# Attention inputs laid out by numpy ahead of a windowed-attention and mixture-of-experts kernel

## The chip, the cores and the metric

The kernel runs on one core of one Trainium2 chip. The metric is the device time of one execution in microseconds. The comparison is with the kernel before the change, of which three timed runs and one profiled execution are at hand. What numpy does to the inputs before the launch and to the output after it is not in the device time.

## The reference

Three layers follow one another. The first is attention with 4 batches, 8 heads, 576 positions and 64 features to a head. Heads 0 to 3 see the last 32 positions, heads 4 to 7 see every fourth of the last 128. The second layer is a mixture of 8 experts that takes 2304 tokens of 512 features, picks two experts for each token by noisy logits and sums their outputs. The third is a dense pair of matrices with a softmax gate and a normalization between them.

```python
scores = scale * np.matmul(q, k.transpose(0, 1, 3, 2))
rel = pos[:, None] - pos[None, :]
mask_plain = (rel >= 0) & (rel < 32)
mask_dil = (rel >= 0) & (rel < 128) & (rel % 4 == 0)
scores = np.where(masks, scores, -1e9)
attn = np.exp(scores - max); attn = attn / (attn.sum + 1e-9)
x = np.matmul(attn, v)                       # (4, 8, 576, 64) -> 2304 tokens x 512

logits = x @ w_gate
noisy = logits + np.log1p(np.exp(x @ w_noise)) * noise
top2 = the two largest of 8
out[t] = sum over top2 of weight * (relu(x[t] @ w1[e]) @ w2[e])

h = out @ w_in
solu = h * softmax(h)
y = layernorm(solu) * g_ln @ w_out
```

The dilated heads read every fourth position. If positions are sorted by their remainder modulo 4 (their class, 144 positions each), the dilated window becomes a plain window of 32 neighbours inside a class. Both kinds of head are then computed by the same code on blocks of 64 queries and 96 keys, with a mask.

## The kernel before

**Attention.** A *pair* j is two heads of one batch; there are 16 of them, four to a batch, in the order of heads given by `HPS`. A pair has three *groups* of three blocks of 64 queries, so there are 48 groups. For group g the kernel runs these steps:
- `scores(g)` on PE: two matmuls add the mask (L191), twelve matmuls multiply queries and keys (L196), into one of two PSUM buffers `s`;
- `soft_a(g)`: DVE takes the maxima (L203), ACT the exponentials with their sums (L207);
- `soft_0(g)` and `soft_b(g)`: DVE adds 1e-9 and takes the reciprocal (L212, L217), POOL multiplies (L219, tile `pn`);
- `ptrans(g)`: PE transposes the probabilities (L226), ACT copies them out of PSUM (L228);
- `pv(g)`: twelve matmuls with the values (L243), and `evac` copies the result into `xt` on DVE (L263), one copy for a plain pair, two for a dilated one.

The loop over g is a software pipeline written out by hand: iteration g issues `scores(g + 2)`, `ptrans(g - 1)` and `pv(g - 2)` on PE in this order, and each engine works through its own instructions in program order.

**Inputs.** q and k come from DRAM as rows of 64 features (`load_qk`, four transfers to a pair, L139, tile `nat`). `trans(j, part)` turns them: four parts to a pair, each of three PE transposes of 96 columns (L167); ACT copies the keys out (L177), DVE the queries with the scale (L179), into `qkt`, which has room for two pairs. For dilated pairs the copy also sorts positions by class. The table `TD` puts two parts each into the second and third iteration of a pair. v comes in rows of 64 features too (`load_v`, L147 for plain heads, L155 for dilated ones, tile `vwt`); a block needs 96 keys, of which 32 are the last ones of the block ahead, and `share_v` copies these on POOL (L160). All these loads are issued on SP's queue.

**Beside the groups.** From g = 15 on, `gate(n)` computes a tile of 128 tokens for the router: six matmuls or more into `ga_a`, two into `ga_b` (L288), and the rows are stored to DRAM (L303). From g = 23 on, the router's DVE work (`front`, `rank`) is spread over the iterations from a list `bg` by a table of costs, and from g = 26 on the first expert's weights are split in two parts by ACT and POOL (L564, L567). 13 of the 18 gates stand inside the loop. After it come the other gates, the second half of the routing, and then the experts (L610), which begin at about 161 us and fill PE from about 180 us to the end.

Of the kernel before, what the change touches and what calls it, by code (L numbers as in the profile page):

```python
# [24 lines left out]
W = 32  # L25
# [8 lines left out]
N1 = 9  # L34
NR = 9
# [7 lines left out]
TD = ((), ((2, 0), (2, 2)), ((2, 1), (2, 3)))  # L43
# [13 lines left out]
XE_ = lambda g: g > 50  # L57
# [3 lines left out]
def const_arrays():  # L61
# [20 lines left out]
    bits = (masks.reshape(128, -1).view(np.uint32) >> 16).astype(np.uint16)  # L82
    return {"masks": bits, "cpack": pk}

# [6 lines left out]
def tile_kernel(ctx, tc, q, k, v, w_gate, w_noise, noise, w1, w2, w_in, w_out, g_ln, masks, cpack, out, stop=None):  # L91
# [33 lines left out]
    qk = big.tile([128, 2, 2 * S + W], F32, name="qkt", tag="ha")  # L125
    QT = [qk[:, i, :S] for i in range(2)]
    KT = [qk[:, i, S:] for i in range(2)]
    NAT = {}
    XT = {}

    def load_qk(j, halves=(slice(0, 6),)):
        b, hp = j // 4, HPS[j % 4]
        if j not in NAT:
            NAT[j] = big.tile([128, 2, 6, 2 * D], F32, name="nat", tag=("x0", "x1h", "x1l")[j % 3])
        o = (b * H + 2 * hp) * S * D
        for g in halves:
            for i, src in enumerate((q, k)):
                for h in range(2):
                    nc.sync.dma_start(NAT[j][:96, i, g, D * h:D * h + D],  # L139
                                      dram_ap(src, o + (h * S + g.start * 96) * D,  # L140
                                              [[D, 96], [96 * D, g.stop - g.start], [1, D]]))

    def load_v(b, d, i0=0, i1=NBLK):
        o = (b * H + 4 * d) * S * D
        if d == 0:
            for h in range(4):
                nc.sync.dma_start(VW[0][W:, i0:i1, h], dram_ap(v, o + (h * S + 64 * i0) * D,  # L147
                                                               [[D, 64], [64 * D, i1 - i0], [1, D]]))
            return
        u = 64 * i0  # L150
        while u < 64 * i1:
            c = u // NCLS
            e = min(64 * (u // 64 + 1), (c + 1) * NCLS)
            p0 = W + u % 64
            nc.sync.dma_start(VW[1][p0:p0 + e - u, u // 64],  # L155
                              dram_ap(v, o + (DIL * (u - c * NCLS) + c) * D, [[DIL * D, e - u], [S * D, 4], [1, D]]))
            u = e

    def share_v(d, i0, i1):
        nc.gpsimd.tensor_copy(VW[d][:W, i0 + 1:i1 + 1], VW[d][64:64 + W, i0:i1])  # L160

    def trans(j, part):
        hp = HPS[j % 4]
        nm, a = part // 2, part % 2
        ps = psum.tile([128, 288], F32, name="tr", tag="t")
        for g in range(3):
            nc.tensor.transpose(ps[:, 96 * g:96 * g + 96], NAT[j][:96, nm, 3 * a + g], idf[:96, :96])  # L167
        if hp < 2:
            src = ps
            place = lambda t: t[:, 288 * a:288 * a + 288]  # L170
        else:
            src = ps.rearrange("p (i c) -> p c i", c=4)
            place = lambda t: t.rearrange("p (c i) -> p c i", c=4)[:, :, 72 * a:72 * a + 72]

        def evac():
            if nm == 1:
                nc.scalar.copy(place(KT[j % 2][:, W:]), src)  # L177
            else:
                nc.vector.tensor_scalar(place(QT[j % 2]), src, scale, None, op0=OP.mult)  # L179

        return evac
# [707 lines left out]
    for p_ in (0, 2):  # L889
        trans(0, p_)()  # L890
# [288 lines left out]
```

## Time and profile before

| what | value |
|---|---|
| median of 3 runs | 861.88 us (861.49 to 861.94) |
| the profiled execution's own time | 860.89 us |
| span of its trace | 859.1 us |
| PE busy | 827.4 us, 96% of the span |
| DVE, ACT, POOL busy | 531.7, 337.6 and 197.1 us |
| TensorE clock granted, mean | 0.985 |

The profiled execution's time is 1.8 us more than the span, and 1.0 us less than the median. Shares of busy time over the whole span say little about the first 150 us, where attention runs and the limits change from stage to stage. The rows that matter are therefore those of stretches of that part. Groups are numbered here from 0, and a group's start is the start of its mask matmuls (L191).

### The profile page before, as it was taken

How to read it: one execution, taken by the hardware profiler on the slowest of the kernel's cores; microseconds unless marked ns; L12 is line 12 of the kernel's file. 1: busy time of each engine (PE TensorE's matmuls, PEld its weight loads, DVE VectorE, ACT ScalarE, POOL GpSimd, SP SyncE). 2: the span in 40 equal slices, each digit the busy share in tenths (PEclk: the TensorE clock that was granted, in tenths of full speed). 3: DMA queues.
4: the chain of work that ended last, by engine and by line, in shares of the span. 5: the costliest groups of instructions: out<-in, count | busy, mean ns of one | idle time of the engine just before them, and what ended most of it. 6: DMA issues, size and time to landing. Idle time of an engine off the chain costs nothing.

```text
span 859.1 us, 14969 instructions
## 1 busy us (share of the span) xinstructions
PE 827.4 (96%) x5588; PEld 722.5 (84%) x5588; DVE 531.7 (62%) x1289; ACT 337.6 (39%) x862; POOL 197.1 (23%) x212
## 2 busy tenths in 40 slices
PE   6999888999999999999999999999999999999997
PEld 4877767889998998988989989889987888888886
DVE  2656688735475564755855755341656878777883
ACT  2767757424332322432323223331534433443332
POOL 3533557351101001011010020011314222212200
PEclk9999969899999999999999999999999999999999
DMA  7668774334445525545455364252522222122101
GB/s 167 127 131 195 181 182 132 112 97 130 133 158 172 184 91 192 167 142 170 149 193 170 101 197 148 67 154 75 160 76 84 74 74 61 56 68 74 39 25 40
DMA packets 113470, 106.23 MB, mean 124 GB/s; under 512 B 65744, under 2 KB 86256, under 8 KB 113392
## 3 DMA queue, kind: packets, MB, share of 16 engines
q1 hardware_dynamic: 107248, 85.25, 34.3%
q0 software_dynamic: 6144, 19.96, 7.9%
q8 instruction: 46, 0.75, 0.4%
q14 instruction: 32, 0.26, 0.1%
HBM read 81.00 MB, written 24.19 MB: 122 GB/s over the span
## 4 chain that ended last, share of the span: by engine, by line
PE 86%; DVE 6%; DMA 3%; SPq 2%; ACT 1%; issue 1%; POOL 0%; POOLq 0%; ACTq 0%; DVEq 0%
PE l L610 51%; PE fh L738 11%; PE fo L610 10%; PE xtp L597 2%; DMA nat<-in_k_dram 2%; PE pv L243 2%; PE s L196 2%; PE fzp L756 2%; PE tr L167 2%; PE pt L226 2%; PE ga_a L288 1%; SPq L139 1%; SPq L147 1%; PE xtp L676 1%; PE s L191 1%
## 5 line engine op out<-in xcount | busy, mean ns | idle before, releaser
L580 POOL DMA_INDIRECT xg<-xs,idx x40 | 46.3, 1158 | 329.7 <-PE xtp L597 323.3
L610 PE MATMUL l<-x,w1h 128*128 128x256 f32 x512 | 95.4, 285 | 0.0
L610 PE MATMUL l<-x1h,w1h 128*128 128x384 f32 x256 | 85.9, 335 | 0.0
L610 PE MATMUL l<-x1l,w1h 128*128 128x384 f32 x256 | 85.8, 335 | 0.0
L610 PE MATMUL l<-x1h,w1l 128*128 128x384 f32 x256 | 85.6, 335 | 0.0
L610 PEld LDWEIGHTS l<-x,w1h 128*128 128x128 f32 x512 | 83.1, 193 | 0.6
L610 PE MATMUL l<-w2h,h1h 128*128 128x512 f32 x192 | 76.8, 400 | 0.0
L610 PE MATMUL l<-w2h,h1l 128*128 128x512 f32 x192 | 75.1, 391 | 0.0
L610 PE MATMUL l<-w2l,h1h 128*128 128x512 f32 x192 | 74.9, 390 | 0.0
L610 PE MATMUL l<-x,w1l 128*128 128x256 f32 x256 | 72.9, 285 | 0.0
L631 DVE SCALAR_TENSOR_TENSOR h1l<-l,h1h 128x384 fp32r<-128x384 f32 x64 | 35.4, 553 | 47.2 <-ACT h1h L630 47.1
L630 ACT ACTIVATE h1h<-l 128x384 fp32r<-128x384 f32 x64 | 31.4, 491 | 83.0 <-PE l L610 83.0
L567 DVE TENSOR_TENSOR w1l<-raw,w1h 128x1024 fp32r<-128x1024 f32 x32 | 38.3, 1230 | 28.1 <-ACT w1h L564 28.1
L650 DVE COPY yo<-l 128x512 f32<-128x512 f32 x22 | 15.2, 692 | 64.6 <-PE l L610 64.6
L207 ACT ACTIVATE p<-s,ng 128x96 f32<-128x96 f32 x144 | 47.2, 339 | 14.7 <-DVE r L212 9.0
L610 PE MATMUL fo<-w2x,fz 128*128 128x512 f32 (+1 forms) x228 | 52.8, 379 | 0.0
L610 PE MATMUL l<-w2h,h0h 128*128 128x512 f32 x128 | 50.8, 397 | 0.0
L630 ACT ACTIVATE h0h<-l 128x256 fp32r<-128x256 f32 x58 | 22.3, 384 | 71.3 <-PE l L610 71.0
L738 PE MATMUL fh<-w1h,fx 128*128 128x512 f32 x144 | 49.1, 403 | 1.2 <-ACT fx L682 0.7
L610 PE MATMUL l<-w2h,h0l 128*128 128x512 f32 x128 | 50.1, 391 | 0.0
L670 POOL TENSOR_TENSOR yg<-yg 128x512 f32<-128x512 f32 x18 | 23.2, 1292 | 116.8 <-ACT yg L669 116.8
L610 PE MATMUL l<-w2l,h0h 128*128 128x512 f32 x128 | 50.0, 390 | 0.0
(204 smaller groups left out, 2023.6 us busy)
## 6 DMA issues: line engine op xcount, KB each, us to landing
raw<-in_moe_w_dram SPq DMA_DIRECT2D x64, 512.0 KB, 3.9
ys<-yo SPq DMA_DIRECT2D x40, 256.0 KB, 2.1
out_dram<-yo SPq DMA_DIRECT2D x17, 256.0 KB, 2.0
nat<-in_q_dram SPq DMA_DIRECT2D x30, 144.0 KB, 3.5
nat<-in_k_dram SPq DMA_DIRECT2D x30, 144.0 KB, 3.7
raw<-in_moe_w_in_dram SPq DMA_DIRECT2D x8, 512.0 KB, 4.1
raw<-in_moe_w_out_dram SPq DMA_DIRECT2D x8, 512.0 KB, 3.7
xs<-xo SPq DMA_DIRECT2D x13, 256.0 KB, 3.7
```

Of the source, the lines that this page charges most:

```text
L167: nc.tensor.transpose(ps[:, 96 * g:96 * g + 96], NAT[j][:96, nm, 3 * a + g], idf[:96, :96])
L196: nc.tensor.matmul(ps[h, i], QT[j % 2][h, u:u + 64], KT[j % 2][h, u:u + 96], start=False, stop=i == 2, skip_group_check=True)
L207: nc.scalar.activation(p[:, i], s[:, i], AF.Exp, bias=ng[:, i:i + 1], accum_out=sm[:, i:i + 1])
L226: nc.tensor.transpose(ps[:, i], pn[:, i], idf)
L243: nc.tensor.matmul(ps[64 * h:64 * h + 64, 64 * i:64 * i + 64], vw[:, 3 * t + i, 2 * (hp % 2) + h, :], pt[:, i, 64 * h:64 * h + 64], start= ...
L567: (eng or nc.vector).tensor_sub(l, r, h.bitcast(F32))
L580: nc.gpsimd.indirect_dma_start(out=t, out_offset=None, in_=xs[:128 * N1] if h == 0 else xs, in_offset=bass.IndirectOffsetOnAxis(ap=idx[:, ...
L610: nc.tensor.matmul(ps, A[x], Bm[y], start=first and i == 0, stop=last and i == 2)
L630: nc.scalar.activation(hh[:, ft], ps, AF.Relu)
L631: nc.vector.scalar_tensor_tensor(hl[:, ft], ps, 0.0, hh[:, ft].bitcast(F32), op0=OP.max, op1=OP.subtract)
L670: nc.gpsimd.tensor_tensor(a, a, b, op=OP.add)
L738: nc.tensor.matmul(ps, FX[n][x][:, kk], W1[y][:, 2 * c:2 * c + 2, kk], start=kk == 0 and i == 0, stop=kk == 3 and i == 2)
```

## The change

Numpy now lays out the inputs before the launch, in `lay_out`:
- q and k are given as one array `kq`: for each pair, 128 rows (two heads of 64 features), each with 576 key positions and then 576 query positions. Dilated heads have their positions sorted by class. `load_kq` brings a pair with one transfer, two pieces of 2304 bytes to a row, into one of four buffers `kq` (before: rows of 256 bytes, transposed on PE).
- v is given as blocks of 96 keys, with the 32 shared keys written out twice. `load_v` brings all nine blocks of four heads with one transfer; `share_v` is gone.
- The order of tokens in the rest of the kernel is by class for all heads. Plain pairs are written to `xt` with a permutation in the `evac` copy, dilated ones with one plain copy. The noise is permuted in the same way, and the output is put back by numpy.
- The identity for the mask matmul is part of the `masks` array, and the gate weights come as one array.

On chip, `trans` and its copies on ACT and DVE are gone. `scale_q` multiplies a pair's queries by the scale in place on DVE, once to a pair, in the iteration of a pair's first group, one pair ahead. A new function `heat` runs matmuls of a tile of ones: 34 ahead of group 0's scores, and 16 after those of group 1. Nothing reads their result.

```diff
+H0, H1 = 34, 16
-TD = ((), ((2, 0), (2, 2)), ((2, 1), (2, 3)))
...
+    KQ = [big.tile([128, W + 2 * S], F32, name="kq", tag=t) for t in ("x0", "x1h", "x1l", "ha")]
+    KT = [t[:, :W + S] for t in KQ]
+    QT = [t[:, W + S:] for t in KQ]
...
+    def load_kq(j, u0=0, u1=S):
+        o = (j // 4 * 4 + HPS[j % 4]) * 128 * 2 * S
+        dst = KQ[j % 4][:, W:].rearrange("p (a s) -> p a s", a=2)[:, :, u0:u1]
+        nc.sync.dma_start(dst, dram_ap(kq, o + u0, [[2 * S, 128], [S, 2], [1, u1 - u0]]))
+
+    def scale_q(j, eng, u0=0, u1=S):
+        eng.tensor_scalar(QT[j % 4][:, u0:u1], QT[j % 4][:, u0:u1], scale, None, op0=OP.mult)
...
+        o = (2 * b + d) * 96 * NBLK * 4 * D
+        nc.sync.dma_start(VW[d][:, i0:i1].rearrange("p i h d -> p (i h d)"),
+                          dram_ap(vw, o + i0 * 4 * D, [[NBLK * 4 * D, 96], [1, (i1 - i0) * 4 * D]]))
...
         if hp < 2:
-            evs = [(x[:, hp, 192 * t:192 * t + 192], ps)]
+            dst = x[:, hp].rearrange("p (c i) -> p c i", c=DIL)[:, :, 48 * t:48 * t + 48]
+            src = ps.rearrange("p (i c) -> p c i", c=DIL)
         else:
...
+            dst, src = x[:, hp, 192 * t:192 * t + 192], ps
...
+    def heat(n):
+        ps = psum.tile([128, 128], F32, name="heat", tag="t")
+        for _ in range(n):
+            nc.tensor.matmul(ps, one, one, start=True, stop=True, skip_group_check=True)
+
+    heat(H0)
+    scale_q(0, nc.vector, 0, 192)
     scores(0)
-    for p_ in (1, 3):
-        trans(0, p_)()
+    soft_a(0)
+    scale_q(0, nc.vector, 192, S)
     scores(1)
-    soft_a(0)
+    heat(H1)
...
-        if t == 0:
+        if t == 0 and j + 1 < 16:
+            scale_q(j + 1, nc.vector)
             if j + 3 < 16:
-                load_qk(j + 3)
-        for dj, p_ in TD[t]:
-            if 2 <= j + dj < 16 and j + dj > 1:
-                ev.append(trans(j + dj, p_))
...
-        if g and vb < 4:
-            if m < 3:
-                load_v(vb, d, 3 * m, 3 * m + 3)
-            else:
-                share_v(d, max(3 * m - 10, 0), 3 * m - 7)
+        if g >= 8 and g % 6 == 2 and g < 45:
+            load_v((g - 8) // 12 + 1, (g - 8) // 6 % 2) if g < 42 else None
```

**PE, one iteration in the middle of a pair.** Before, between a group's scores (`s`) and the transposes of the probabilities (`pt`) stand six transposes of inputs (`tr`):

```order
L191 LDWEIGHTS idb
L191 MATMUL s<-mk,idb 64x288
L191 LDWEIGHTS idb
L191 MATMUL s<-mk,idb 64x288
L196 MATMUL s<-qkt 64x96 x6
L167 MATMUL tr<-cp,nat 128x96 x6
L226 MATMUL pt<-cp,pn 96x128 x3
L243 MATMUL pv<-ptS,vwt 64x64 x6
```

The same iteration of the changed kernel:

```order
L171 LDWEIGHTS mk
L171 MATMUL s<-mk 64x288
L171 LDWEIGHTS mk
L171 MATMUL s<-mk 64x288
L176 MATMUL s<-kq 64x96 x6
L206 MATMUL pt<-cp,pn 96x128 x3
L223 MATMUL pv<-ptS,vwt 64x64 x6
```

The six transposes are gone and the rest stands in the same order (the program lists two matmuls of the two heads as one row).

**DVE, two iterations early in the loop.** Before, each copy of queries out of PSUM (`qkt<-tr`) stands between the copy of a result and the next maxima:

```order
L263 COPY xt<-pv 128x192
L179 TENSOR_SCALAR qkt<-tr 128x4x72
L203 TENSOR_REDUCE ng<-s 128x3
L212 TENSOR_SCALAR r<-sm 128x3
L217 RECIPROCAL r<-r 128x3
L263 COPY xt<-pv 128x192
L179 TENSOR_SCALAR qkt<-tr 128x4x72
L203 TENSOR_REDUCE ng<-s 128x3
```

The changed kernel at the first group of a pair and the one after it:

```order
L232 COPY xt<-pv 128x4x48
L156 TENSOR_SCALAR kq<-kq 128x576
L183 TENSOR_REDUCE ng<-s 128x3
L192 TENSOR_SCALAR r<-sm 128x3
L197 RECIPROCAL r<-r 128x3
L232 COPY xt<-pv 128x4x48
L183 TENSOR_REDUCE ng<-s 128x3
```

Two operations that read PSUM have become one that reads and writes SBUF (`kq<-kq`), and it waits for the transfer of the next pair.

**SP, the loads of the first iterations.** Before:

```order
L147 DMA vwt<-in_v_dram 64x3x64 x4
L139 DMA nat<-in_q_dram 96x6x64 x2
L139 DMA nat<-in_k_dram 96x6x64 x2
L147 DMA vwt<-in_v_dram 64x6x64 x4
L139 DMA nat<-in_q_dram 96x6x64 x2
L139 DMA nat<-in_k_dram 96x6x64 x2
```

In the changed kernel the same part of the queue, from the first blocks of v to the third pair, with the rest of the constants (`cp`) in it:

```order
L160 DMA vwt<-in_vw_dram 96x768
L153 DMA kq<-in_kq_dram 128x1152
L160 DMA vwt<-in_vw_dram 96x1536
L759 DMA cp<-in_cpack_dram 128x316
L153 DMA kq<-in_kq_dram 128x1152
```

Sixteen transfers have become four, and over the whole of attention 160 transfers of q, k and v have become 26.

## Rows read from the trace of the kernel before

**Rows 1.** The page: its first line.

```profile
span 859.1 us, 14969 instructions
```

**Rows 2.** Windows by stage: window, length, busy time of each engine, clock, DMA share, GB/s.

```profile
0.00:24.55 24.55, 16.19 (x126) 12.60 (x126) 6.30 (x22) 8.12 (x33) 7.97 (x20) 1.00 0.78 160
24.55:51.43 26.88, 24.79 (x400) 20.14 (x397) 16.63 (x61) 19.32 (x93) 12.35 (x18) 0.99 0.59 119
51.43:98.36 46.93, 43.61 (x590) 35.80 (x589) 28.81 (x116) 33.24 (x147) 20.25 (x28) 0.97 0.75 170
98.36:145.96 47.60, 41.74 (x541) 34.08 (x541) 39.39 (x153) 30.00 (x126) 30.67 (x33) 0.86 0.66 165
145.96:180.00 34.04, 29.55 (x287) 26.31 (x287) 25.53 (x110) 15.94 (x47) 14.54 (x18) 0.90 0.31 99
```

**Rows 3.** Timeline of PE: start, length, instructions; mask matmuls of groups, two score rows.

```profile
21.35 1.17 PE L196 MATMUL s<-qkt 64*64 64x96 f32 x12
...
24.55 0.31 PE L191 MATMUL s<-mk,idb 64*64 64x288 bf16 x2
...
24.69 0.66 PE L196 MATMUL s<-qkt 64*64 64x96 f32 x12
...
26.24 0.31 PE L191 MATMUL s<-mk,idb 64*64 64x288 bf16 x2
...
28.45 0.31 PE L191 MATMUL s<-mk,idb 64*64 64x288 bf16 x2
...
51.43 0.45 PE L191 MATMUL s<-mk,idb 64*64 64x288 bf16 x2
...
95.48 0.31 PE L191 MATMUL s<-mk,idb 64*64 64x288 bf16 x2
...
98.36 0.31 PE L191 MATMUL s<-mk,idb 64*64 64x288 bf16 x2
...
145.96 0.31 PE L191 MATMUL s<-mk,idb 64*64 64x288 bf16 x2
```

**Rows 4.** The chain that ended last, in order of time: start, length, what.

```profile
15.58 4.10 DMA nat<-in_k_dram
...
44.80 3.77 DMA vwt<-in_v_dram
...
74.28 5.72 DMA nat<-in_k_dram
...
83.08 6.57 DMA nat<-in_k_dram
```

**Rows 5.** Groups by line and form, 0 to 180 us: busy, mean ns, idle before, releasers.

```profile
L167 PE MATMUL tr<-cp,nat 96*128 96x96 f32 x192 | 27.9, 286 | 11.9 <-DMA nat<-in_q_dram 5.5 <-DMA nat<-in_k_dram 5.5 <-DVE qkt L179 0.6
...
L179 DVE TENSOR_SCALAR qkt<-tr 128x288 f32<-128x288 f32 x32 | 14.6, 457 | 30.3 <-PE tr L167 30.1
L160 POOL COPY vwt<-vwt 32x768 f32<-32x768 f32 x16 | 13.0, 813 | 15.8 <-DMA vwt<-in_v_dram 15.2
L177 ACT COPY qkt<-tr 128x288 f32<-128x288 f32 x32 | 12.8, 400 | 9.4 <-PE tr L167 9.4
...
L263 DVE COPY xt<-pv 128x192 f32<-128x192 f32 x24 | 8.3, 344 | 3.2 <-PE pv L243 3.1
...
L263 DVE COPY xt<-pv 128x144 f32<-128x144 f32 x16 | 6.5, 408 | 0.0
...
L263 DVE COPY xt<-pv 128x48 f32<-128x48 f32 x16 | 3.9, 241 | 1.3 <-PE pv L243 1.3
```

**Rows 6.** DMA rates in 40 slices: of 10 to 20 us, then of 210 to 220 us.

```profile
GB/s 92 161 193 218 193 257 256 257 247 211 228 195 204 167 162 120 197 193 116 191 122 157 226 210 219 234 182 251 261 281 263 237 193 183 166 224 236 219 195 208
...
GB/s 393 139 25 16 197 246 311 213 33 82 139 16 74 188 344 328 393 434 426 434 254 33 16 33 0 0 0 0 0 115 180 164 328 238 238 360 402 344 344 279
```

**Rows 7.** DVE on SBUF: a group after 180 us; line 212 alone (min/median/max ns).

```profile
L522 DVE TENSOR_SCALAR nt<-nt 128x512 int32<-128x512 int32 x16 | 6.7, 418 | 0.0
...
L212 DVE TENSOR_SCALAR r<-sm x48: 152/160/1212, 11.1 to 150.0; 128x3 f32<-128x3 f32 x48
```

More of the change, by code (lines that the diff above doesn't have):

```diff
@@ L81, in const_arrays, with by_class, lay_out @@
     pk[:, CP_VAL:CP_VAL + 36] = 128 * (np.arange(36)[None, :] // 2) + r[:, None] - TOK0
-    bits = (masks.reshape(128, -1).view(np.uint32) >> 16).astype(np.uint16)
+    masks = np.concatenate([np.eye(128, dtype=np.float32), masks.reshape(128, -1)], 1)
+    bits = (masks.view(np.uint32) >> 16).astype(np.uint16)
     return {"masks": bits, "cpack": pk}
+def by_class(a, axis):
+    s = a.shape
+    a = a.reshape(s[:axis] + (NCLS, DIL) + s[axis + 1:])
+    return np.ascontiguousarray(np.swapaxes(a, axis, axis + 1)).reshape(s)
+def lay_out(given):
+    q, k, v, noise = (given.pop(n) for n in ("q", "k", "v", "moe_noise"))
+    half = lambda a: np.concatenate([a[:, :H // 2], by_class(a[:, H // 2:], 2)], 1)
+    kq = np.stack([half(a).reshape(B, H // 2, 2, S, D).transpose(0, 1, 2, 4, 3) for a in (k, q)], 4)
+    vp = np.pad(half(v), ((0, 0), (0, 0), (W, 0), (0, 0)))
+    rows = 64 * np.arange(NBLK)[None, :] + np.arange(96)[:, None]
+    vw = vp[:, :, rows].reshape(B, 2, 4, 96, NBLK, D).transpose(0, 1, 3, 4, 2, 5)
+    nz = by_class(noise.reshape(B, S, E), 1).reshape(NT, 128, E).transpose(1, 0, 2)
+    wg = np.stack([given.pop(n) for n in ("moe_w_gate", "moe_w_noise")], 1).reshape(4, 128, 16).transpose(1, 0, 2)
+    given.update(kq=kq.reshape(B * H // 2, 128, 2 * S), vw=vw.reshape(B * 2, 96, NBLK * 4 * D),
+                 noise=nz.reshape(128, NT * E), gates=wg.reshape(128, 64))
 def dram_ap(t, offset, dims):
@@ L90, in tile_kernel @@
 @with_exitstack
-def tile_kernel(ctx, tc, q, k, v, w_gate, w_noise, noise, w1, w2, w_in, w_out, g_ln, masks, cpack, out, stop=None):
+def tile_kernel(ctx, tc, kq, vw, gates_w, noise, w1, w2, w_in, w_out, g_ln, masks, cpack, out, stop=None):
     nc = tc.nc
@@ L143, in load_v @@
-    def load_v(b, d, i0=0, i1=NBLK):
[L144 to L157, printed above, removed]
@@ L195, in scores @@
             for h in hd:
-                nc.tensor.matmul(ps[h, i], QT[j % 2][h, u:u + 64], KT[j % 2][h, u:u + 96], start=False,
+                nc.tensor.matmul(ps[h, i], QT[j % 4][h, u:u + 64], KT[j % 4][h, u:u + 96], start=False,
                                  stop=i == 2, skip_group_check=True)
@@ L912, in tile_kernel @@
         late = []
-        ev = []
-        if g == 0:
-            for p_ in range(4):
-                trans(1, p_)()
-        if t == 0:
+        if t == 0 and j + 1 < 16:
+            scale_q(j + 1, nc.vector)
             if j + 3 < 16:
-                load_qk(j + 3)
-        for dj, p_ in TD[t]:
-            if 2 <= j + dj < 16 and j + dj > 1:
-                ev.append(trans(j + dj, p_))
+                load_kq(j + 3)
         if 0 < g <= NG:
             ptrans(g - 1)
-        for f in ev:
-            f()
         if g > 1:
@@ L1157 @@
 _INS = ["q", "k", "v", "moe_w_gate", "moe_w_noise", "moe_noise", "moe_w1", "moe_w2", "moe2_w_in", "moe2_w_out", "moe2_g_ln"]
+_ARGS = ["kq", "vw", "gates", "noise", "moe_w1", "moe_w2", "moe2_w_in", "moe2_w_out", "moe2_g_ln", "masks", "cpack"]
 def kernel(**inputs):
@@ L1168 @@
             given[name] = given[name].view(np.int64)
+    lay_out(given)
     given.update(const_arrays())
     arrays, args = {}, []
-    for name, a in given.items():
+    for name in _ARGS:
+        a = np.ascontiguousarray(given[name])
         arrays[f"in_{name}_dram"] = a
@@ L1177 @@
     r = _run(nc, [arrays], core_ids=[0])
-    return r.results[0]["out_0_dram"]
+    rows = r.results[0]["out_0_dram"].reshape(B, DIL, NCLS, DM)
+    return np.ascontiguousarray(rows.transpose(0, 2, 1, 3)).reshape(N, DM)
```

107 lines of the change are left out of this document (25 added, 82 removed).

## The prediction

> **What bounds the kernel now.** The span is 859.1 us [rows 1]; the profiled execution took 860.89 us, 1.8 us more. I first looked at the chain that ended last: behind about 180 us it is PE matmuls of the experts and nothing that the change touches, so that a microsecond won ahead of that comes out at the end, if the experts start earlier by it. So I cut the time ahead of it into stages at the starts of groups 5, 17, 33 and 47 [rows 3] and asked for each what set its pace [rows 2].
>
> *Stage A*, to 24.55 us: PE works 16.19 of it. The chain shows a transfer of keys of 4.10 us that ends just ahead of the first dense stretch [rows 4]. The granted clock reads 1.00, yet the same twelve score matmuls take 1.17 us at 21.35 and 0.66 us at 24.69 [rows 3]; I go by the durations and call the first the low level (1.2 GHz of 2.4).
> *Stage B*, twelve groups in 26.88 us: PE is busy for 24.79. From group 5 to 6 it is 1.69 us, from 6 to 7 it is 2.21 [rows 3]; the difference of 0.52 us is the six input transposes, which stand in two of three iterations. 12 x 1.69 + 8 x 0.52 = 24.4 us; the other 2.4 us go with the 3.77 us wait for v that the chain has at 44.80 [rows 4].
> *Stage C*, 16 groups with 8 gates in 46.93 us. Groups 32 to 33 with a gate take 2.88 us [rows 3], so a gate costs 1.19. 16 x 1.69 + 8 x 1.19 + 10.7 x 0.52 = 42.2; the other 4.7 us are around the two long waits for keys at 74.28 and 83.08 [rows 4].
> *Stage D*, 14 groups in 47.60 us: here DVE is the fullest engine with 39.39 us, because the router's work lies on it, and the clock falls to a mean of 0.86 [rows 2]. With two levels, one half of the other, that is 28% of the stage, 13 us, at 1.2 GHz.
> *Stage E*, 145.96 to 180: last groups, gates, second half of the routing.
>
> **The change part by part.** The input transposes leave PE: 192 matmuls, 27.9 us busy [rows 5], some of it at the low level. With them go 32 copies of 0.400 us on ACT, 32 of 0.457 on DVE, and on POOL the copies of shared v, 16 of 0.813 and 8 smaller ones [rows 5]. Of ACT and POOL I count nothing by itself: in B, ACT is busy 19.32 us [rows 2], less 8 x 0.40 is 16.1, that is 1.34 a group, under PE's 1.69; POOL with 12.35 us is lower still. PE hides both.
>
> *scale_q* on SBUF: a row of the same kind takes 0.418 us for 512 elements [rows 7]; 576 of them at that rate are 0.47 us at most. Two copies of 0.457 become one of 0.47: DVE gains 0.44 a pair. It waits for the next pair's load; behind it on DVE stand a group's maxima, for which ACT waits. With three pairs loaded ahead I count that wait at nothing after the start; without that cover it would be what the chain shows for keys, 4 to 6.6 us a time.
> *evac*: a dilated group had copies of 0.408 and 0.241 us, a plain one 0.344 [rows 5]. All become one; the copies of queries that read PSUM in a permuted order cost no more than the others (one mean of 0.457, 32 of one form [rows 5]), so I take 0.344 for both. That is 0.30 us for every second group.
> *heat*: no row shows such a matmul. A pair of mask matmuls of 288 columns takes 0.45 us at the low level and 0.31 at the high one [rows 3]; 128 columns of it are 0.20 and 0.14 us. Lower still are the score matmuls, 0.66/12 = 0.055 us each. The 34 last 4.7 us by the middle value, the 16 last 2.2. I take 0.14, the pure matmul row that is nearest in size.
> The Trainium skill (TensorE: Matmul & The Clock Gate, part 1) states 107 ns for each such matmul from cold and 56 ns later: an estimate of 34 x 0.107 + 16 x 0.056 = 4.5 us for all 50 instead of 6.9, which would make the sum 2.4 us better.
>
> Now the stages.
> *A.* Heat from 1 us (an allowance for the start), group 0 at 5.7, group 1 at 7.4, heat to 9.6, and three groups of 1.69: group 5 at 14.7 instead of 24.55, a gain of **9.9 us**. Ends: with everything low, heat is 10 us and a group 1.69 x 1.17/0.66 = 3.0, group 5 starts at 26, a loss of 1.5; with heat at 0.055 each it is a gain of 14.
> *B.* 12 x 1.69 = 20.3 us: a gain of **6.6**. Ends 2.4 (only the wait goes and another engine holds the old pace) and 6.6.
> *C.* 16 x 1.69 + 8 x 1.19 = 36.6 us; ACT would have 33.24 - 10.7 x 0.40 = 29.0, DVE about 26. I add 2 us of waits, as PE and ACT are both near full there: 38.6, a gain of **8.3**. Ends 4.7 (only the waits for loads go) and 10.3.
> *D.* DVE: 39.39 - 9.3 x 0.457 + 4.7 x 0.47 - 7 x 0.30 = 35.2 us of work. Before, it idled 8.2 us; I leave 5.8 of it, since its waits for PE get shorter: 41.0 us, a gain of **6.6**. PE would need 14 x 1.69 and five gates, 29.6 us, at the high level. Ends: 0 (routing sets the pace as it did) and 12.4 (DVE never idle).
> *E.* The order of work there is the same: **0**, ends -1 and +1.
> Sum 9.9 + 6.6 + 8.3 + 6.6 = 31.4 us: a span of 827.7, 829.5 as the profile counts a time, and against the median of 861.88 it is **830.5 us**.
>
> The loads have to keep up. To group 33, at 73.6 us by this sum, the queue has to bring 13 pairs of 0.59 MB, 6 pieces of v of 0.885, 0.8 of constants, 5 weights of 0.52, and store 8 tiles of 0.26: 18.5 MB, or 251 GB/s. From 10 to 20 us, rows of 256 bytes moved at a mean of about 200 GB/s with slices up to 281; from 210 to 220, where rows are 1 KB and 2 KB, the fullest slices run at 393 to 434 [rows 6]. The new rows of 2304 and 9216 bytes are nearer to the second, so I count transfers at nothing behind the start.
>
> **Rivals.**
> *The loads set the pace.* If the queue stays at 210 GB/s, 18.5 MB take 88 us, and with 2 us for the start group 33 comes at 90 instead of 73.6: 16 us of the gain are lost, **847 us**. For it: v is read one and a half times now. Against it: rows 6.
> *DVE and POOL keep each other out.* Line 212 works on three numbers for each partition, mostly in 0.16 us, but at times takes 1.21 [rows 7]; it waits a microsecond for something that is no input. If each of the 16 scale_q, now from SBUF to SBUF, loses 1.05 us so or makes POOL's `pn` lose it, that is 17 us, if all lies on the path **847**, with half of it **839 us**. For it: 0.418 us for 512 elements against 0.457 for 288 from PSUM [rows 5, 7] is a faster mode. Against it: DVE has 0.4 us of slack a group in B and C, which takes most of it.
> The Trainium skill (SBUF — State Buffer, section on its two separate sides) has this as a rule against the change: a DVE instruction in a two-port mode and a GpSimd instruction share one port pair, and the one that comes second is blocked for the whole of the first. By that rule the 839 us would be the time; line 212's worst case is a wait that fits it.
> *The clock falls.* With fewer matmuls a group, and DVE setting the pace in D, PE idles more there. If all of D runs low, its 14 groups of 3.0 and five gates of 2.1 are 52.5 us, 11.5 more than forecast: **842 us**. The form that ends on the other side: from group 5 to 47 PE has 42 groups and 13 gates, 86.5 us at the high level and 153 at the low one. Before, that took 121.4; with the 9.9 us of stage A the change is slower from 131.3 us on, that is with two thirds of this work at 1.2 GHz, and with all of it the time is **884 us**. For it: D at 0.86 [rows 2]. Against it: B and C at 0.99 and 0.97 with PE busy for 92 to 93%, and without the waits for loads that stood in them.
> The Trainium skill (TensorE: Matmul & The Clock Gate, part 1) says that idle stretches make the clock fall and that activity lifts it; which of both D will be, no row here shows.
>
> **How the numbers follow.** Forecast 72%, loads 8%, ports 8%, clock low in D 8%, clock low in most of attention 4%. The time is the forecast's. If all upper ends of the gain met (14, 6.6, 10.3, 12.4, 1) it would be 818 us, if all lower ones, 857; ends on one side rarely meet, so I take 819 below, and 846 above, which holds the clock in D, half the ports and nearly the loads. About 2 in 10 lie outside. A measurement of this kernel can tell some 0.2%, 1.7 us, from no change. Faster than that: 95%; within it 1%, a chance meeting of several lower ends; slower 4%, the clock.
>
> **What would show it.** In the changed trace: group 0's mask matmuls near 5.7 us, and the twelve score matmuls at 0.66 us from group 2 on; groups 1.69 us apart in B and no chain piece of `kq` or `vwt` transfers of over 2 us behind the first groups; a gate still at 1.19 us; group 17 near 35, 33 near 74 and 47 near 115 us; DVE over 85% busy in D; the experts' part as long as before. It is wrong if a transfer ends waits of PE in C, if scale_q's mean is over 0.7 us, if the clock in D is under 0.86, or if the groups of B are over 1.8 us apart though no load is late, since then another engine's chain had held them.

## The result, and the profile after

The changed kernel took 831.44 us (median of four runs, 827.85 to 832.71) against 861.91 us for the kernel before on the same chip: a ratio of 0.9641, 95% interval 0.9616 to 0.9667. The profiled execution is the fastest of its four, 827.85 us, with a span of 826.1 us against 859.1 [rows 1]. The forecast was 830.5 us.

The same cut by stage as in [rows 2], at the starts of groups 5, 17, 33 and 47; columns are window, length, busy time (and count) of PE, weight load, DVE, ACT and POOL, then granted clock, DMA share and GB/s:

```profile
0.00:13.26 13.26, 10.42 (x138) 8.95 (x139) 4.55 (x20) 6.24 (x28) 2.45 (x9) 1.00 0.82 251
13.26:34.37 21.11, 20.59 (x354) 15.97 (x350) 15.13 (x54) 17.29 (x85) 8.96 (x15) 1.00 0.82 239
34.37:71.26 36.89, 36.65 (x533) 29.54 (x530) 28.31 (x104) 30.24 (x136) 14.85 (x20) 1.00 0.84 258
71.26:114.12 42.86, 37.06 (x494) 29.75 (x493) 39.42 (x144) 27.69 (x118) 26.49 (x27) 0.84 0.59 181
```

PE's timeline, to lay beside [rows 3] (start, length, instructions; in brackets the idle time ahead and what ended it):

```profile
1.01 3.81 PE L856 MATMUL heat<-one 128*128 128x128 bf16 x34 [1.01 <-POOL base L749]
...
7.70 1.07 PE L856 MATMUL heat<-one 128*128 128x128 bf16 x16
...
13.26 0.31 PE L171 MATMUL s<-mk 64*64 64x288 bf16 x2
14.96 0.31 PE L171 MATMUL s<-mk 64*64 64x288 bf16 x2
...
34.37 0.31 PE L171 MATMUL s<-mk 64*64 64x288 bf16 x2
37.24 0.31 PE L171 MATMUL s<-mk 64*64 64x288 bf16 x2
```

Read it as a table of gains against [rows 2]:

| stage | before | after | gain | forecast |
|---|---|---|---|---|
| A, to group 5 | 24.55 | 13.26 | 11.3 | 9.9 |
| B, groups 5 to 16 | 26.88 | 21.11 | 5.8 | 6.6 |
| C, groups 17 to 32 | 46.93 | 36.89 | 10.0 | 8.3 |
| D, groups 33 to 46 | 47.60 | 42.86 | 4.7 | 6.6 |
| E, group 47 to the end | 713.1 | 712.0 | 1.2 | 0 |
| sum | 859.1 | 826.1 | 33.0 | 31.4 |

In C, PE is busy for 36.65 of 36.89 us: nothing is left there but PE's own work. Groups in B are 1.70 us apart (13.26 to 14.96), a group with a gate takes 2.87 (34.37 to 37.24). B has one late load, the fourth pair, which group 9's scores need (the 0.53 us ahead of 20.88): it is the last piece of a transfer over 1 us in the chain of waits up to 150 us (start, length, what):

```profile
7.95 12.39 DMA kq<-in_kq_dram
20.37 0.47 DVE kq L156
20.88 0.71 PE s L176 x12
```

A was something else in the kernel before. From 0.76 to 15.54 us its chain is SP, which issues one transfer after another at 0.39 to 0.73 us each (lines 139 and 147 alone make half of A); behind the last of these stands the transfer of keys at 15.58 us [rows 4]. In the changed kernel five issues stand in the chain, to 3.76 us.

```profile
6.20 0.73 SPq L147
...
15.04 0.51 SPq L139
```

### The profile page after: what moved, and what is told of

Same layout as the page of the kernel before. It is cut to its first block, busy times and chain, and to the rows that moved or that the text cites. A ratio compares the mean times of both kernels' runs of the same rounds, so it can differ in the third digit from the quotient of the medians.

```text
span 826.1 us, 14343 instructions
## 1 busy us (share of the span) xinstructions
PE 804.3 (97%) x5446; PEld 702.6 (85%) x5446; DVE 527.1 (64%) x1251; ACT 328.1 (40%) x830; POOL 178.2 (22%) x184
## 4 chain that ended last, share of the span: by engine, by line
PE 87%; DVE 8%; DMA 2%; ACT 1%; issue 1%; SPq 0%; ACTq 0%; DVEq 0%
PE l L579 53%; PE fh L707 11%; PE fo L579 11%; PE xtp L566 2%; PE fzp L725 2%; PE pv L223 2%; PE s L176 2%; DMA kq<-in_kq_dram 2%; PE ga_a L257 1%; PE pt L206 1%; PE xtp L645 1%; PE s L171 1%; DVE hot L424 1%; DVE ng L183 1%; DMA vwt<-in_vw_dram 1%
## 5 line engine op out<-in xcount | busy, mean ns | idle before, releaser
L599 ACT ACTIVATE h1h<-l 128x384 fp32r<-128x384 f32 x64 | 31.4, 491 | 83.2 <-PE l L579 83.2
L187 ACT ACTIVATE p<-s,ng 128x96 f32<-128x96 f32 x144 | 47.2, 337 | 19.7 <-DVE r L192 12.3
L617 ACT COPY yo<-l 128x512 f32<-128x512 f32 x18 | 10.6, 587 | 99.7 <-PE l L579 96.1
```

The costliest lines, as they stand in the source:

```text
L187: nc.scalar.activation(p[:, i], s[:, i], AF.Exp, bias=ng[:, i:i + 1], accum_out=sm[:, i:i + 1])
L599: nc.scalar.activation(hh[:, ft], ps, AF.Relu)
```

## The experiments

All start from the changed kernel; a ratio is against the kernel before, run beside it. The times of one group of runs on a chip (the first four, the next four, the last four) are compared with each other first; only the first group has the changed kernel itself among its runs. "E0" is the changed kernel once more.

**E0, the changed kernel again.** No edit.

> The changed kernel itself, unaltered, as the measure for the other runs on this chip. Expected 831 us (ratio 0.964 to the kernel before), and that its runs differ by some 4 us, more than those of the kernel before. The profiled execution that I read was at the low end (827.9 us). If the spread lies in stage D, where DVE and POOL hold each other up for up to 1.3 us at a time, the profile of this run has groups 5, 17 and 33 at the same times as the first (13.3, 34.4 and 71.3 us, within 0.5), and only group 47 (114.1) moves.

Median 830.92 us (0.9635, 0.9609 to 0.9662). The profiled span is 828.7 us, 2.6 more than in the run above. Its group 10 starts at 25.44 instead of 22.49, while C is 36.89 again and D is the same within 0.15 us in every engine:

```profile
74.21:117.08 42.87, 36.94 (x493) 29.68 (x493) 39.44 (x144) 27.71 (x118) 26.47 (x27) 0.84 0.59 181
```

So the 2.6 us between these two profiles come from the first 25 us, where loads hold PE up, and not from D, where I had looked for them; E1 and E9, which leave D alone, have 42.87 and 42.89 there too. In this run A gained 9.2 us, B 4.9, C 10.0, D 4.7 and E 1.5, together 30.4; A and B are under the forecast. Over the profiles with the same start (the first, E0, E5, E7 and E8) group 17 comes between 34.4 and 37.3 us, so that a single profile's value for A and B together is good to some 3 us.

**E1, no heat.**

```diff
-    heat(H0)
...
-    heat(H1)
```

> Both calls of heat left out, 50 matmuls that nothing reads; all else as in the change. If the ones keep the PE at its high level through the start: groups 0 to 4 run at the low level, 3.0 us a group instead of 1.7, group 5 starts 3 to 5 us later than at 13.3 us, and the time is 3 to 5 us over the change's. If the loads set the pace of the start anyway (the trace of the change has a chain piece of 12.4 us of query and key loads up to 20.3 us, and group 10 waits for it): group 5 is later, but group 10 still starts at 22.5, and the time is the change's within 1 us. If heat is in the way of group 0: group 0 starts near 4.1 instead of 4.75.

831.58 us (0.9647, 0.9619 to 0.9675), 0.7 us over E0 and within the interval. Group 5 starts 1.2 us later than in E0 (16.52), less than two runs of the same kernel differ by; group 10 starts at 25.63 against 25.44. PE's timeline shows the cost: without heat the groups' mask matmuls stay at 0.45 us until group 5, then go to 0.31.

```profile
16.52 0.45 PE L171 MATMUL s<-mk 64*64 64x288 bf16 x2
...
18.85 0.31 PE L171 MATMUL s<-mk 64*64 64x288 bf16 x2
```

The fourth pair can be scaled at 23.32 us in E0 and at 23.02 in E1. E0's PE waits 1.27 us for it, E1's is never idle from group 5 to group 10, so that here the faster start is waited away. A worth of heat is not shown: 0.7 us is less than the interval's 2 us to either side, and where the fourth pair comes earlier (20.37 us in the first profile) it may be more.

**E2, the transposes back on PE alone.** 180 transposes of 96x96 (before: 192, the 12 others ahead of the loop) write to a tile that nobody reads; no copies come back.

```diff
+    def idle_t():
+        ps = psum.tile([128, 288], F32, name="tr", tag="t")
+        for i in range(3):
+            nc.tensor.transpose(ps[:, 96 * i:96 * i + 96], idf[:96], idf[:96, :96])
...
+        if g == 0 or t > 0 and j + 2 < 16:
+            for p_ in range(4 if g == 0 else 2):
+                idle_t()
```

> The change, with as many PE transposes as before (three of 96 columns for a part, two parts in the second and third iteration of a pair, four in the first iteration) put back at their places; they turn a constant tile, nothing is copied out of PSUM, and the loads are the new ones. If PE's own work set the pace in stages B and C: two of three groups take 2.2 us instead of 1.7, B is 4.2 us longer, C 5.6, D 0 to 3 because DVE holds it, the start 1: 11 to 14 us over the change. If what was won came from the waits for loads and the copies alone, the time stays within 3 us of the change's.

840.81 us (0.9753, 0.9718 to 0.9789): 9.9 us over E0. Windows of B, C and D, columns as above:

```profile
15.74:40.67 24.93, 24.54 (x400) 20.10 (x396) 14.44 (x53) 17.47 (x85) 9.14 (x16) 1.00 0.67 191
40.67:82.34 41.67, 41.67 (x592) 34.64 (x588) 26.94 (x104) 30.21 (x136) 14.92 (x21) 1.00 0.76 227
82.34:126.07 43.73, 37.55 (x541) 30.82 (x541) 39.06 (x144) 27.44 (x118) 25.93 (x27) 0.96 0.57 177
```

Against E0, B is 2.9 us longer, C 4.8 and D 0.9. The lengths of B and C are within 0.6 us of those that the prediction built from PE's own work in the kernel before, 24.4 and 42.2 us. PE's share of the gain is thus about 10 of 30 us, most of it in B and C, a little less than the 11 to 14 expected. D, with 48 matmuls more, hardly notices them.

**E3, the same layout in rows of 256 bytes.** The host leaves a gap behind each 64 numbers of `kq` and `vw`, so that the same bytes move in many short pieces, from rows with gaps between them; on chip nothing changes but the loads, and their number stays (the first pair, loaded in two parts, takes four).

```diff
+        o = (j // 4 * 4 + HPS[j % 4]) * 128 * 18 * 80
+            nc.sync.dma_start(dst.rearrange("p a s d -> p (a s) d"), dram_ap(kq, o, [[18 * 80, 128], [80, 18], [1, D]]))
...
+                          dram_ap(vw, o + i0 * 4 * 80, [[NBLK * 4 * 80, 96], [80, (i1 - i0) * 4], [1, D]]))
```

> The change, with the same bytes of query, key and value laid out in DRAM as runs of 256 bytes with gaps of 64 bytes between them, so that every load moves in pieces of 256 bytes as before; same number of transfers, same places in SBUF. The rival on the loads: at some 210 GB/s the 18.5 MB up to group 33 take 88 us, group 33 starts near 90 instead of 71.3, and the time is near 847 to 850 us, with PE waiting for kq and vwt transfers in B and C. If the length of the rows does not matter and only the number of transfers does: within 2 us of the change.

843.29 us (0.9782, 0.9737 to 0.9827), 12.4 us over E0. Windows of B, C and D, then two pieces of its chain of waits:

```profile
17.07:44.22 27.15, 22.17 (x351) 17.10 (x349) 14.58 (x53) 17.46 (x85) 8.90 (x15) 0.94 1.10 186
44.22:81.11 36.89, 36.65 (x532) 29.54 (x528) 28.09 (x104) 30.18 (x136) 14.84 (x20) 1.00 1.13 218
81.11:129.39 48.28, 38.08 (x494) 30.21 (x494) 39.59 (x144) 28.14 (x119) 26.91 (x27) 0.82 0.85 197
```

```profile
18.00 10.71 DMA kq<-in_kq_dram
...
78.81 6.38 DMA xs<-xo
```

The queue is full (a share of 1.10 and 1.13) at 186 and 218 GB/s, where the long rows carry 239 and 258 at 0.82 and 0.84. A is 1.8 us longer than in E0, B 5.2, D 5.4, and C is the same to the hundredth: the time goes in two stalls, one ahead of group 10 for keys and one behind group 33, where a store of `xs` stands in the chain until 85.19 us. So in this kernel the long rows are worth about as much as the transposes. Their length is not the only thing that differs: E3's pieces start every 320 bytes, those of the kernel before at multiples of 256, and in the kernel before the transfers moved 160 and 170 GB/s in A and C at shares of only 0.78 and 0.75 [rows 2], fewer busy engines to the byte than in E3. A part of the 12.4 us may be the price of the gaps; no run separates it. The prediction's rival of late loads (847 us at 210 GB/s) comes near to this kernel in time, not to the changed one; but it had group 33 at 90 us, where 81.11 was measured, and the rest was lost in D.

**E4, the scaling of queries on ACT.**

```diff
-            scale_q(j + 1, nc.vector)
+            q_ = QT[(j + 1) % 4]
+            nc.scalar.activation(q_, q_, AF.Copy, scale=scale)
```

> The change, with the scaling of each further pair's queries (line 156, one instruction a pair) moved from DVE to ACT. On DVE the 15 of them took 10.8 us, 0.72 each instead of 0.46 because some are held up while POOL works, four of them with 3.0 us in stage D. If DVE's work sets the pace in D: D is 1 to 3 us shorter and the time 1 to 3 us under the change's 831. If ACT is too full for them in C (30.2 of 36.9 us, and about 0.6 us more for each of five pairs): C grows by 0 to 2 us and the time is the change's or 1 us over.

831.01 us (0.9663, 0.9624 to 0.9702). DVE has 36.27 us of work in D instead of 39.42, and D takes 43.42 us, 0.6 longer; C is 0.25 shorter. What `scale_q` costs on DVE is covered, and DVE's total is not what D waits for, unless ACT's 1.9 us of work more there (29.59 against 27.69) took the gain back, which this run does not separate.

**E5, the first weights' split on DVE.** POOL subtracts for the experts' first weights (`w1l`, `w2l`) while the later groups run; here DVE does it.

```diff
-    first = [item(key, 2, nc.gpsimd) for key in stream[:8]]
+    first = [item(key, 2, nc.vector) for key in stream[:8]]
```

> The change, with the subtractions of the first expert's weight split (16 halves, 1.3 us each on POOL) on DVE instead, where one of this size takes 0.69 us elsewhere in the trace. DVE gets about 11 x 0.69 = 7.6 us more work in stage D. If DVE instructions of stage D are long because POOL holds them up (line 192 at a mean of 0.405 us instead of 0.159, and single router instructions at 1.15 to 1.29 us instead of 0.2, some 9 us together): these fall back to 0.16 to 0.2 us, D stays within 2 us of 42.9, and the time within 2 us of the change's. If they are long by themselves: D is 7 to 8 us longer and the time 838 to 839 us.

828.46 us (0.9615, 0.9582 to 0.9648), 2.6 under E4; the intervals overlap, with those of the changed kernel too. D is 41.77 us: POOL falls from 26.5 to 15.5 us there and DVE, with nine subtractions more, from 39.4 to 37.1. DVE's groups in D, of the changed kernel and then of E5 (count, busy us, mean ns, idle ahead):

```profile
L192 DVE TENSOR_SCALAR r<-sm 128x3 f32<-128x3 f32 x14 | 5.7, 405 | 0.0
...
L156 DVE TENSOR_SCALAR kq<-kq 128x576 f32<-128x576 f32 x4 | 3.0, 744 | 0.0
```

```profile
L192 DVE TENSOR_SCALAR r<-sm 128x3 f32<-128x3 f32 x13 | 4.2, 319 | 0.0
L536 DVE TENSOR_TENSOR w1l<-raw,w1h 128x512 fp32r<-128x512 f32 x5 | 3.9, 776 | 0.0
L536 DVE TENSOR_TENSOR w2l<-raw,w2h 128x512 fp32r<-128x512 f32 x4 | 3.4, 839 | 0.0
...
L156 DVE TENSOR_SCALAR kq<-kq 128x576 f32<-128x576 f32 x4 | 2.0, 503 | 0.0
```

DVE was given 7.3 us of subtractions, and its other instructions became some 9 us shorter in all: 405 to 319 ns, 744 to 503. The "busy" of DVE in D holds waits for POOL. How that looks is seen in the changed kernel's timeline of both engines, around three of the splits:

```profile
76.56 1.44 POOL L536 TENSOR_TENSOR w1l<-raw,w1h 128x512 fp32r<-128x512 f32 x1
76.80 1.25 DVE L326 TENSOR_SCALAR rw<-ru 128x40 f32<-128x40 f32 x1
...
86.58 1.26 POOL L536 TENSOR_TENSOR w1l<-raw,w1h 128x512 fp32r<-128x512 f32 x1
86.75 1.15 DVE L356 TENSOR_TENSOR m<-oh 128x40 bf16<-128x40 f32 x1
...
89.42 1.33 POOL L536 TENSOR_TENSOR w1l<-raw,w1h 128x512 fp32r<-128x512 f32 x1
89.55 1.29 DVE L382 SCALAR_TENSOR_TENSOR rw<-ra,cp 128x72 f32<-128x72 f32 x1
```

Each DVE instruction starts while POOL's runs and ends with it (78.00 and 78.05, 87.84 and 87.90, 90.75 and 90.84). In E5, without POOL's subtractions, the same three take 170, 201 and 220 ns. The Trainium skill (SBUF — State Buffer, the section on its two separate sides) says that a GpSimd instruction and a DVE one that needs the port pair the two share lock each other out: the one that starts first has the pair for its whole length, and the other is blocked. These rows agree.

**E6, the split earlier.** The first weights are split from iteration 14 on, 12 iterations sooner, and loaded as much sooner, so most of it falls into C.

```diff
-WG, WS = 26, (0, 1, 2)
+WG, WS = 14, (0, 1, 2)
...
-    for g in (20, 21, 22):
+    for g in (8, 9, 10):
```

> The change, with the first expert's weight loads at iterations 8, 9 and 10 (20, 21, 22) and the split of its weights from iteration 14 (26) on; ACT and POOL do the same work, 12 iterations sooner, so that about four of its halves stand in stage D instead of eleven. If POOL's halves hold up DVE in D: D is 4 to 6 us shorter, at 37 to 39 us, B and C hardly change because DVE idles 6 and 8.6 us there, and the time is near 826 us. If the loads cannot take 2 to 3 MB more in B and C (239 and 258 GB/s at a share of 0.82 and 0.84): PE waits for kq or vwt there, and the gain is lost or turned into a loss of 1 to 4 us.

829.95 us (0.9645, 0.9612 to 0.9679). D falls to 41.39 us with DVE at 36.12 and the clock at 0.92, C rises to 38.73. The loss moves with the split (eleven of its halves stand in C now, five in D instead of nine): 1.5 us out of D, 1.8 into C. No wait of PE for a load stands in C, so it is not the queue, which moves 279 GB/s there at a share of 0.90.

**E7, matmuls of ones in D.** Ten behind the last matmuls of each of the iterations 33 to 47, 120 of them in D, to keep the clock up.

```diff
+        if 33 <= g < 48:
+            heat(10)
```

> The change, with ten matmuls of ones more (heat) in each iteration from 33 to 47, behind the matmuls with the values; nothing reads them. In D the granted clock is 0.84 on the mean, about 14 us at 1.2 GHz. If the low clock costs time in D: the clock rises to 0.95 or more, groups 38 to 44 come closer together, and D is 3 to 6 us shorter. If DVE sets the pace: the clock rises as well, but D stays within 1 us of 42.9, since PE's longer matmuls hid behind DVE; the time is within 1 us of the change's.

832.77 us (0.9673, 0.9636 to 0.971). Window of D:

```profile
73.32:118.43 45.11, 40.60 (x613) 33.44 (x612) 39.24 (x146) 28.13 (x120) 27.41 (x28) 0.96 0.60 184
```

The clock is at 0.96 instead of 0.84, and D is 2.2 us longer. The ones cost PE time of their own (busy 40.60 us instead of 36.94), so this run alone does not settle it; but D runs at 0.92 in E4 and at 0.96 in E2, and is no shorter in either. The low clock in D goes with PE's idle time and is not what the stage waits for.

**E8, no routing work between the groups.** The second part of the router and those after it (`front`, `rank`, `xtrans` of the first tiles) leave the loop and come behind it; with DVE's work go some 45 small matmuls of D on PE and POOL's part.

```diff
-    at(FB, lambda: bg.extend((front(0, 4, N1), rank(0, N1, 9, 3, early))))
-    at(XA, lambda: late.append(xtrans(0, 0, True)))
-    at(XA + 1, lambda: late.append(xtrans(0, 1, True)))
-    if N2 > N1:
-        at(FC, lambda: bg.append(front(N1, N1, N2)))
...
+    bg.extend((front(0, 4, N1), rank(0, N1, 9, 3, early), front(N1, N1, N2)))
...
+    xtrans(0, 0)
+    xtrans(0, 1)
```

> The change, with the router's DVE work of iterations 32 to 47 (two parts of front, and rank) taken out of the loop and put right behind it, the first two gathers' transposes too. Nothing is left out, but the experts start later, so the whole time will be 5 to 15 us over the change's; what is asked is the length of stage D alone. If the router's work among the groups sets the pace there: D is 14 groups of 1.69 and six gates of 1.19, 31 us instead of 42.9, at a clock of 0.97 or more, although the first expert's weight split still stands in it. If the weight split on POOL and ACT sets it: D stays over 38 us.

Window of D:

```profile
72.24:102.77 30.53, 29.94 (x449) 24.00 (x448) 23.14 (x82) 26.69 (x116) 20.95 (x23) 1.00 0.79 243
```

D is 30.53 us, with PE busy for 29.94 of it at a clock of 1.00, though the weights' split still stands in it, nine halves as before. The prediction's value for PE alone was 29.6, with five gates; the expectation's 31 counted six, one too many. So the router's work between the groups makes the whole of the 12.3 us that D takes longer, the idle time of PE and the low clock included. How it does so is seen in the changed kernel's chain of waits: in a large part of D that is DVE's queue, where a group's maxima (`ng`) and its `r` stand behind steps of the router (`hot`), with few gaps:

```profile
94.58 0.45 DVE ng L183
95.03 1.14 DVE r L192
...
96.98 1.29 DVE hot L416
98.27 0.37 DVE ng L183
...
100.88 2.69 DVE hot L424 x4
103.57 0.37 DVE ng L183
```

Behind group 47 that work stands bare: the first expert matmul comes at 136.51 us against 130.57 in E0, and the time is 837.5 us (0.974, 0.9708 to 0.9771). Hiding it in D at 12.3 us is the better trade.

**E9, another order of the first loads.** The fourth pair is loaded in the prologue, ahead of the second half of v, which comes in three pieces.

```diff
-    load_v(0, 1)
+    load_kq(3)
+    for i_ in (0, 3, 6):
+        load_v(0, 1, i_, i_ + 3)
...
-            if j + 3 < 16:
+            if 0 < j and j + 3 < 16:
```

> The change, with the fourth pair's queries and keys loaded ahead of the values of the dilated heads, and these in three transfers of three blocks. In the change group 10 starts at 22.5 to 25.4 us, from run to run, because the scaling of the fourth pair waits for its load behind 0.89 MB of values that are needed two iterations later. If the order of the loads makes that wait: group 10 starts at 20.5 to 22.5 us and the time is 1 to 3 us under the change's. If the queue is simply full (4.9 MB in 20 us): the wait moves to the values, and group 10 and the time stay where they are, within 1 us.

831.09 us (0.9639, 0.9612 to 0.9665): no gain in the median, and neither outcome in the trace. The wait for the fourth pair is gone: groups 9 and 10 start 1.70 us apart, in E0 3.18. But group 3's scores wait 1.49 us for the second pair, and behind that wait groups 4 to 6 run at the low level (0.45 us for a pair of mask matmuls instead of 0.31), up to 2.98 us apart, with PE busy all the time; so group 10 starts at 26.55, in E0 at 25.44:

```profile
11.96 0.71 PE L176 MATMUL s<-kq 64*64 64x96 f32 x12 [1.49 <-DVE kq L156]
...
16.48 0.45 PE L171 MATMUL s<-mk 64*64 64x288 bf16 x2
...
19.46 0.45 PE L171 MATMUL s<-mk 64*64 64x288 bf16 x2
```

E5, in the old order, has the same wait at the same place (2.29 us) and slow groups behind it; E11, in the new order, waits 1.03 us there, has no slow groups, and starts group 10 at 22.58. What the order is worth by itself stays open; the medians show nothing, here and in E11.

**E10, the copies of shared values back on POOL.** The whole of v is still loaded; 21 of the 24 old copies (14 of 32x768, 7 of 32x512) write the same numbers over it, one iteration later than before.

```diff
+    def share_v(d, i0, i1):
+        nc.gpsimd.tensor_copy(VW[d][:W, i0 + 1:i1 + 1], VW[d][64:64 + W, i0:i1])
...
+        vb, m = divmod(g + 4, 12)
+        d, m = (0, m) if m < 6 else (1, m - 6)
+        if g >= 5 and vb < 4 and m > 2:
+            share_v(d, max(3 * m - 10, 0), 3 * m - 7)
```

> The change, with the copies of the shared values on POOL put back (21 copies of 0.6 to 0.8 us, three in six iterations, one iteration later than before the change; they write the same numbers that stand there already). If POOL's instructions cost DVE time in stage D: the eight or nine copies there make D 1 to 3 us longer, DVE's short instructions longer on the mean, and the time 1 to 3 us over the change's; in B and C DVE and POOL idle enough to hide them, unless a copy waits for a load, with the products of probabilities behind it on POOL. If the copies were hidden in the kernel before: within 1 us of the change everywhere.

838.87 us (0.9742, 0.9719 to 0.9764), 7.8 us over E9 and more than either theory had. C is 0.8 us longer, D 1.3; some 6 us come behind group 47 (717.7 us to the end of the span, 711.6 in E0). POOL's timeline there, then PE's:

```profile
119.65 0.81 POOL L164 COPY vwt<-vwt 32x768 f32<-32x768 f32 x1 [3.04 <-DMA xg<-xs,idx]
```

```profile
122.48 0.88 PE L209 MATMUL pt<-cp,pn 128*96 128x128 f32 x3 [3.63 <-POOL pn L202]
```

POOL stands idle for 3.04 us ahead of one copy, behind it is the last groups' `pn`, and PE waits 3.63 us for that. The wait is put down to the gather's transfer. What exactly the copy waited for was not taken apart, and 2 of the 6 us have no row here. In the kernel before, the last copy stands ahead of the two gathers, and no such wait follows:

```profile
139.40 0.81 POOL L160 COPY vwt<-vwt 32x768 f32<-32x768 f32 x1
...
141.72 1.10 POOL L580 DMA_INDIRECT xg<-xs,idx  x1 [0.16 <-DVE ce L481]
```

Its stage E is 713.1 us, 1.5 over E0's. So of the 6 us at most 1.5 can be part of what the change won; the rest is the price of copies at E10's place.

**E11, E5 and E9 together.**

> The change, with both the subtractions of the first expert's weight split on DVE and the new order of the first loads. By the run with the split on DVE alone (828.5 us, D at 41.8 instead of 42.9) and 1 to 3 us for the loads: 826 us, between 824 and 829. If the order of loads does nothing: 828 to 829.

827.82 us (0.9614, 0.9593 to 0.9635), the lowest median of all, 3.3 us under E9 and 0.6 under E5. Against E9, run beside it, C and D are shorter by 0.3 and 0.9 us (36.58 and 42.00 against 36.89 and 42.89); the rest lies in the start, where profiles of one kernel differ by some 3 us. Its interval overlaps that of the changed kernel, so that it beats it is likely, not shown; that the order of loads adds to E5 is not shown either.

## Why the prediction was right, and where it was not

The forecast of 830.5 us was 0.9 us under the median, and each stage moved in the direction foreseen. That it came so near is in part luck: against E0, C and E gained 3.2 us more than forecast, and A, B and D 4.3 us less. By its steps:

- **A, +9.9: 11.3 in one run, 9.2 in E0.** Group 0 was to start at 5.7 us and came at 4.75 and 4.41. The term for heat was too large: the row gives 3.81 us for 34 and another shows 1.07 for 16, together 4.9 instead of 6.9. The Trainium skill's figure (TensorE: Matmul & The Clock Gate, part 1) gave an estimate of 4.5 us, and was nearer than the row of mask matmuls that I took. The two microseconds did not reach the end: without any heat the time is the same within the interval (E1), so heat could have been left out of the sum. What the forecast does not name is what A was made of, SP issuing many transfers one after another (the chain shown with the result). No run puts their number back (E3 keeps it, and E2 and E3 give back 0.4 and 1.8 us of A), so that the fewer transfers won most of A is argued from the two chains.
- **B, +6.6: 5.8 and 4.9.** The rhythm (1.69 forecast, 1.70 in the rows) came out as worked, and no other engine took PE's place. What is missing is one load of `kq`, by 0.7 to 1.5 us at group 10: a piece of 12.39 us in the chain, which the prediction had said would not be there behind the first groups, so that counting transfers at nothing was a little too bold. The need of 251 GB/s was right: A, B and C move 251, 239 and 258 GB/s at a share of 0.82 to 0.84. With E3's short rows the price would have been 12.4 us.
- **C, +8.3: 10.0.** The 2 us kept back for two nearly full engines were not needed. ACT at 30.24 us does not touch a PE that is busy for 36.65. The rest, 16 x 1.69 + 8 x 1.19 = 36.6, is within 1% of the measured 36.89. E2 gives 4.8 us of the gain to the transposes. For the other 5.2 the trace of the kernel before has 3.0 us of PE's waits for keys in C (below: total, times, longest) and 0.3 for queries, the changed kernel none; what is left goes with its clock of 0.97 there [rows 2], against 1.00. No run brought these waits back in C, not E3 either, whose short rows stalled elsewhere, so this half is read from the traces and not shown by a run.

```profile
PE tr L167 <- DMA nat<-in_k_dram: 3.0, 2, 1.5
```

- **D, +6.6: 4.7.** This is the step that failed. The sum took DVE's work at 35.2 us and left 5.8 idle; DVE is busy for 39.42 and idle for 3.4. The queries' copies in D were 3.6 us and not 4.3 (9.3 copies counted, 8 there), the four scalings take 3.0 us and not 2.2, `evac` gives back 1.5 and not 2.1, and the instructions on three numbers rose from 3.6 to 5.7 us (13 of 279 ns before, row below; 14 of 405 after, row with E5). That last part is at least in part held time, as E5 shows (319 ns without POOL's subtractions), so DVE's busy time was the wrong thing to add up. Nor does DVE's total set D: E4 took 3.2 us from it and D did not shorten; E8 took the router away and D fell to 30.53, PE's own work. What sets it is the router's work among the groups. That it does so as a serial chain in DVE's queue, in which the groups' own steps stand behind the router's, is what the chain with E8 shows for a part of D; no run took single steps of it apart.

```profile
L212 DVE TENSOR_SCALAR r<-sm 128x3 f32<-128x3 f32 x13 | 3.6, 279 | 0.0
```

- **E, 0: 1.2, and 1.5 in E0,** past its upper end of 1; why was not taken apart.
- **`scale_q`.** Its mean over 15 is 719 ns instead of 470:

```profile
L156 DVE TENSOR_SCALAR kq<-kq 128x576 f32<-128x576 f32 x15 | 10.8, 719 | 2.5 <-DMA kq<-in_kq_dram 2.5
L232 DVE COPY xt<-pv 128x192 f32<-128x192 f32 x48 | 16.5, 343 | 3.5 <-PE pv L223 3.0
```

I had named a mean over 0.7 us as a sign of being wrong. The sign appeared and the time held: some take 0.45 or 0.46 us, as forecast, others up to 1.42 (in D 0.74 on the mean, and 0.50 in E5, without POOL's subtractions), and taking the 15 away from DVE won nothing (E4). The copies to `xt` take 343 ns on the mean, the forecast's 344, and all 48 lie between 326 and 359 ns, so the permuted order costs little or nothing.
- **The clock in D** fell to 0.84, under the 0.86 that was named as a sign. E7 and E8 put it behind PE's idle time: with more matmuls the clock came back and D got no shorter; without the router both came back.
- **POOL was counted at nothing,** since PE hides it. By E10 the absent copies are worth up to 2 us in C and D, which the sum put down to loads and PE; of the other 6 us of E10 at most 1.5 can be in the kernel before.

The rivals: late loads is near what E3 shows. The port rival's mechanism is there (the three pairs of rows with E5), at 0.25 us on a `scale_q` instead of 1.05. Behind the start, the low clock stayed within D. The effects of E2, E3 and E10 (9.9, 12.4 and 7.8) add to 30.1 us, near the change's 30.5, but that is chance: by stage they do not fit. Of A's 9.2 us in E0 they give back 2.2 (E2 and E3), of C's 10.0 some 5.6 (E2 and E10), while E3 alone costs D 5.4, more than the change won there. What the runs show is PE's part in B and C, and that rows as short as E3's would have cost 12.4 us; the start, half of C and E are read from traces or open.

## What to carry to other kernels

Cut a kernel at the places where its limit changes and work out a sum for each stage; in a stage where the bound engine is full (C), its own instructions by their measured time gave the new length to 1%. At the start of a kernel look at the queue that issues the transfers, too: their number can be what it waits for. In a stage where a long serial job runs between the steps of a loop, the busiest engine's total is not the bound, and a part of it may be waiting; only taking the job away shows what it costs. And when numpy lays out an input, the rows that a transfer reads, long or in short pieces with gaps, can be worth as much as the work that the layout spares the engines.

## What the runs showed of the hardware

- Three DVE instructions of 40 to 72 elements a partition, 0.17 to 0.22 us in E5, took 1.15 to 1.29 us in the changed kernel, where they began during a POOL subtraction of 128x512, and ended with it. In the profile they count as busy.
- Moving nine subtractions from POOL to DVE in D, 7.3 us of DVE's time, made DVE's busy time there 2.3 us shorter (E5).
- An issue of a transfer of q, k or v took SP 0.42 to 0.73 us in the first 15.5 us of the kernel before.
- In B and C, with rows of 256 bytes and gaps of 64 between them (E3), the transfers moved 186 and 218 GB/s at a share of 1.10 and 1.13; with rows of 2304 and 9216 bytes 239 and 258 at 0.82 and 0.84, and with more weights to load (E6) 272 and 279 at 0.94 and 0.90.
- In E1 the granted clock did not tell the level of the first groups: it reads 1.00 up to group 5 (first of the two windows of E1 below) as behind it, while pairs of mask matmuls took 0.45 us up to there and 0.31 from 18.85 us on. As in [rows 3], durations had to be read.

```profile
0.00:16.52 16.52, 9.41 (x89) 7.34 (x90) 4.49 (x20) 6.70 (x30) 2.98 (x10) 1.00 0.88 236
16.52:25.63 9.11, 9.11 (x147) 7.15 (x145) 6.21 (x21) 6.84 (x34) 3.75 (x8) 1.00 0.75 240
```
